# Three turns of attention in another order on TensorE, and one more pair of the first dense stage by the plain product

## The chip, the cores and the metric

The kernel runs on one core of a Trainium2 chip. The metric is device time in microseconds (us), the median of several runs. A profiled execution gives the trace from which all rows below are read. PE is TensorE, ACT ScalarE, DVE VectorE, POOL GpSimd and SP SyncE; of SP only its queue of transfers is used here.

## What is computed

Attention of 2 batches and 12 heads over 448 positions (head size 64) is followed by two dense blocks on 896 tokens:

```
scores = cap * tanh(q @ k.T / sqrt(64) / cap)
x  = softmax(scores) @ v                # (896, 768)
h  = x @ w_in1     # 768 x 2048         first dense stage
x  = (h * cos(h)) @ w_out1              # second
h  = x @ w_in2                          # third
out = (h * sigmoid(h)) @ w_out2         # fourth
```

All in float32; most products are made of three matmuls on operands split into a rounded part and a rest.

## The kernel before

**Attention** works through 12 pairs of heads, one turn each. For pair p, `S_pe(p, t)` (L229) multiplies q and k for chunk t: three chunks of two matmul groups (L241) and a small one, t = 3 (L245). The result lies in one of three buffers named `sc`, taken in rotation, so `S_pe(p, 3)` takes the buffer of `S_pe(p, 0)` and must wait until `S_tanh(p, 0)` has read it. `S_tanh` (L253) and `S_exp` (L259) run on ACT. `PV(p, steps)` (L271, matmuls on L275) multiplies with v, one step for two chunks; `PV_mixed` (L279) handles the small chunk, `PV_sums` (L289, L293) the row sums, for which DVE first adds chunks in `e_add` (L301). The order of each engine is the order of the text: turn p issues S of pair p + 1, then PV of pair p. Before the first turn stand pair 0's scores, four matmuls on zeros (`warm_up`, L347, L349), and two of pair 0's three PV steps. In the last turn there are no scores left: `PV_mixed`, `PV_sums` and then the three PV steps.

**The dense stages** run under a planner (`run_plan`). `gemm_in`, `gemm_out`, `gemm_sums` and `gemm_last` describe tasks with an engine, an assumed cost, a due time and the buffers they take; the planner simulates the engines and writes out the order of each. `MARGIN` multiplies its costs for ACT and DVE, `NORMS` says when the last two pairs of attention are ready, and the argument of `run_plan` says when ACT, DVE and SP come free after TensorE starts on the dense work. These numbers change the order only. An adding transfer of 384 KB is planned with 0.9 us on POOL, 2.46 of moving (384 x 1.024 / 0.16 ns) and 3.7 of fixed delays. All dense matmuls are recorded on L706, most DVE sums on L639, most ACT copies on L636, and additions done by a transfer on L484.

The first stage's 16 columns of weight tiles are handled in 8 pairs. The first `PLAIN` pairs are multiplied plainly (`half_prods`); for the others, `m1` to `m7` form seven products of half-sized blocks, and DVE, or an adding transfer where `S1E[p]` says so, makes sums of the weight blocks:

```
pe(3 * len(js), go, ...)     # half_prods: 3 matmuls for each of 6 row blocks, 4 times a pair
pe(9, go, ...)               # block_prod: 9 matmuls, 7 times a pair
```

`HALF1[p]` names the buffers that the split blocks of pair p lie in. In the second stage (`gemm_out`) four groups of sums of weight tiles are made by `w_sum`, `WE[n]` naming the engine of the n-th: DVE, or the adding transfer from POOL's queue.

Of the kernel before, what the change touches and what calls it, by code (L numbers as in the profile page):

```python
# [28 lines left out]
F32 = mybir.dt.float32  # L29
# [9 lines left out]
def tile_attention_ffn_ffn(  # L39
# [11 lines left out]
    B, H, S, D = shape  # L51
    DM = out.shape[0]
    DFF = w_in1.shape[0] * 128
    P = 128
# [42 lines left out]
    xt = [[Part(f"x{j}_{b}") for b in range(B)] for j in range(KD)]  # L97

    KMAX = KD
    PLAIN = 2  # L100
    FIRST_IN = [b * HP + n for n in range(HP) for b in range(2)]
    wjobs = []
    for w_in, w_out in ((w_in1, w_out1), (w_in2, w_out2)):
# [66 lines left out]
    with ExitStack() as actx:  # L170
# [3 lines left out]
        ps_o = actx.enter_context(tc.tile_pool(name="ps_o", bufs=1, space=PSUM))  # L174
# [22 lines left out]
        def load(p):  # L197
            if p >= NPT:
                return
            t = ap_.tile([P, PAD + QK], F32, tag="raw", name=f"raw{p}", bufs=3)  # L200
            if p == 0:
                cut = PAD + FIRST
                nc.sync.dma_start(t[:, :cut], qkv[p][:, :cut])
                nc.scalar.dma_start(t[:, cut:], qkv[p][:, cut:PAD + QK])
            else:
                (nc.gpsimd if p > 2 else nc.sync).dma_start(t[:, PAD:], qkv[p][:, PAD:PAD + QK])
            raw[p] = t

        def load_v(p):
            if p >= NPT:  # L210
                return
            vf[p] = ap_.tile([P, NCH, D], F32, tag="vf", name=f"vf{p}", bufs=2)
            (nc.gpsimd if p > 1 else nc.sync).dma_start(vf[p].rearrange("p c d -> p (c d)"), qkv[p][:, PAD + QK:])
# [15 lines left out]
        def S_pe(p, t):  # L229
            if p >= NPT:  # L230
                return
            ps = ps_s.tile([P, 2, 512], F32, tag="sc", name=f"sc{p}_{t}")
            sc[p, t] = ps
            h, l = qh.get(p), ql.get(p)
            ops = ((h, h), (h, l), (l, h))
            if t < 3:
                cols = slice(S + t * P, S + (t + 1) * P)
                for m, (kk, qq) in enumerate(ops):
                    for u in range(2):
                        rows = slice(u * D, (u + 1) * D)  # L240
                        nc.tensor.matmul(ps[:, u, :S], kk[rows, cols], qq[rows, :S], start=m == 0, stop=m == 2)  # L241
            else:
                x = raw[p][:, PAD:]
                for c in range(0, P, W):
                    nc.tensor.matmul(ps[c:c + W, 0, :S], x[:, FULL + c:FULL + c + W], x[:, :S], start=True, stop=True)  # L245

        def S_tanh(p, t):
            if p >= NPT:
                return
            if t == 0:  # L250
                e32[p] = ap_.tile([P, NCH, S], F32, tag="e32", name=f"e32_{p}", bufs=2)
            n = 2 if t < 3 else 1
            nc.scalar.activation(out=e32[p][:, 2 * t:2 * t + n, :], in_=sc.pop((p, t))[:, :n, :S], func=AF.Tanh, scale=scap)  # L253
# [9 lines left out]
        def acc(d, p, tag):  # L263
            if p in d:
                return d[p], False
            t = ps_o.tile([P, 512], F32, tag=tag, name=f"{tag}{p}") if p < NPT - 1 or tag == "po" else ps_s.tile([P, 2, 512], F32, tag="sc", name=f"{tag}{p}")[:, 0]
            d[p] = t[:, :S]
            return d[p], True


        def PV(p, steps, last=False):  # L271
            po, first = acc(po_, p, "po")
            for n, t in enumerate(steps):
                for u in range(2):
                    nc.tensor.matmul(po[u * D:(u + 1) * D], vf[p][:, 2 * t + u, :], e32[p][:, 2 * t + u, :],  # L275
                                     start=first and n == 0, stop=last and n == len(steps) - 1)


        def PV_mixed(p, last=False):  # L279
            po, first = acc(po_, p, "po")  # L280
            sm, _ = acc(sm_, p, "sm")
            for u in range(2):
                rows, other = slice(u * D, (u + 1) * D), slice((1 - u) * D, (2 - u) * D)
                e = e32[p][rows, NCH - 1, :]
                nc.tensor.matmul(po[rows], vf[p][rows, NCH - 1, :], e, start=first, stop=last)  # L285
                nc.tensor.matmul(sm[other], ones[rows, Q:], e, start=True, stop=False)  # L286


        def PV_sums(p):  # L289
            sm, _ = acc(sm_, p, "sm")  # L290
            x = e01.pop(p)
            for c, e in enumerate((x[:, 1], e32[p][:, 5, :], x[:, 0], e32[p][:, 4, :])):
                nc.tensor.matmul(sm[c * Q:(c + 1) * Q], ones[:, :Q], e, start=False, stop=True)  # L293
# [3 lines left out]
        def e_add(p):  # L297
            if p >= NPT:
                return
            e01[p] = ap_.tile([P, 2, S], F32, tag="e01", name=f"e01_{p}", bufs=2)  # L300
            nc.vector.tensor_tensor(out=e01[p], in0=e32[p][:, 0:2, :], in1=e32[p][:, 2:4, :], op=ALU.add)  # L301
# [3 lines left out]
        def evac(p):  # L305
            xu[p] = ap2.tile([P, S], F32, tag="xu", name=f"xu{p}", bufs=4)
            nc.vector.tensor_copy(xu[p], po_.pop(p))
# [39 lines left out]
        def warm_up(n, ps):  # L347
            for _ in range(n):
                nc.tensor.matmul(ps, zero[:, :P], zero, start=True, stop=True)  # L349
# [27 lines left out]
        S_exp(0, slice(4, NCH))  # L377
        qk_split(1)
        e_add(0)
        warm_up(4, ps_o.tile([P, 512], F32, tag="sm", name="warm1")[:, :S])  # L380
        PV(0, [0, 1])
        for p in range(NPT):
            load(p + 3)
            if p > 0:
                load_v(p + 1)
            for t in range(3):
                S_pe(p + 1, t)
                S_tanh(p + 1, t)
            S_pe(p + 1, 3)
            S_tanh(p + 1, 3)  # L390
            S_exp(p + 1)
            recip(p - 2)
            if p > 0:
                e_add(p)
            qk_split(p + 2)
            for f, *a in early.get(p, []):
                f(*a)
            norm_mul(p - 3)
            norm_split(p - 3)
            if p < NPT - 1:  # L400
                PV(p, [0, 1, 2] if p else [2])
                PV_mixed(p, True)
                evac(p)
                PV_sums(p)
                evac_sums(p)
            else:
                PV_mixed(p)
                PV_sums(p)
                evac_sums(p)
                PV(p, [0, 1, 2], True)  # L410
                evac(p)
        recip(NPT - 2)
        norm_mul(NPT - 3)
# [52 lines left out]
        return t  # L466

    SPARE = 1000
    MARGIN = 1.01

    def dma(eng, kb, fn, r, w, adds=False, **k):
        rate = 0.16 if adds else 0.38 if kb > 450 else 0.24
# [3 lines left out]
    def act(n, fn, r, w, **k):  # L476
        do("ACT", MARGIN * (90 + 0.84 * n), fn, r, w, **k)

    def dve(n, fn, r, w, one=False, **k):
        do("DVE", MARGIN * (66 + 1.05 * n), fn, r, w, **k)  # L480

# [127 lines left out]
                    if not v.left:  # L609
                        give_buf(v)  # L610

    NORMS = 6900, 9700
    GE, WE, LE = [["DVE", "DMA"][n] for n in (0, 0, 0, 1)], [["DVE", "DMA"][n] for n in (0, 0, 0, 1)], [["DVE", "DMA"][n] for n in (1, 1)]
    FE = "DVE"
    S3E = [["DVE", "DMA"][n] for n in (1, 1, 1, 0, 0, 0, 0, 0)]
    DUE = [220000, 230000, 240000, 250000, 260000, 270000, 280000, 290000, 300000, 310000, 320000, 330000, 1000000000, 1000000000, 1000000000, 1000000000]
    base_s = KF + 4 * (HK + 1)
    base_l = base_s + KF

    S1E = [["DVE", "DMA"][n] for n in (1, 0, 1, 0, 0, 0, 0, 0)]  # L620
    HALF1 = [('half', 'ring'), ('half', 'half'), ('half', 'half'), ('half', 'ring'), ('ring', 'ring'), ('half', 'ring'), ('half', 'half'), ('ring', 'ring')]
    low, high = range(KD - 2), range(KD - 2, KD)
    PLAIN_ORDER = [(0, 0), (1, 0), (2, 0), (0, 1, low), (1, 1, low), (0, 1, high), (1, 1, high), (2, 1)]
    for n in range(3, 2 * PLAIN):
        PLAIN_ORDER += [(n, 0), (n, 1)]
    ORDER1 = []
    for p in range(PLAIN, HP):
        q = p - PLAIN
        ORDER1 += [(1, p), (5, p)] + ([(7, p - 1)] if q else []) + [(2, p), (6, p)] + ([(4, p - 1)] if q else []) + ([(7, p)] if p == HP - 1 else []) + [(3, p)]
# [30 lines left out]
    def convert(i, out, outs, view, due=1e9, pool="raw"):  # L660
# [14 lines left out]
        k = {"due": due}  # L675
        do("ACT", MARGIN * 800, f_word, [], [raw], **k)
        do("ACT", MARGIN * 800, f_scale, [], [raw], **k)
        dve(n, f_join, [raw], outs, **k)

    def split(n, hi, lo, vhi, vlo, src, r, neg=False):  # L680
        if n < 800:
            def go():
# [4 lines left out]
                else:  # L687
                    nc.vector.tensor_copy(vhi(), src())
            t = do("COPY", MARGIN * (90 + 0.84 * n), go, r, [hi])
            t.other = 100 + 0.5 * n  # L690
# [227 lines left out]
    def gemm_in():  # L918
# [14 lines left out]
        for j in range(KD):  # L933
            for b in range(B):
                TX[f"B{j // HK + 1}{b + 1}", j % HK] = made(xt[j][b])
        for p, at in ((NPT - 2, NORMS[0]), (NPT - 1, NORMS[1])):
            x, (_, *pair) = v[p - NP][1], TX["B22", p - NP - HK]
# [14 lines left out]
        def start(p):  # L952
            blk[p], rest[p] = blocks((2 * p, 2 * p + 1), p, Val("dbl", I32), True, S1E[p], HALF1[p])

# [79 lines left out]
        every = range(KD)  # L1034
        ws = [plain(i) for i in range(2 * PLAIN)]
        pts = {}
# [198 lines left out]
    gemm_out()  # L1235
    gemm_sums()
    gemm_last()
    run_plan({"ACT": 2200, "DVE": 4000, "SP": 7500})


# [46 lines left out]
```

## Time and profile before

| | |
|---|---|
| median of 3 runs | 514.46 us (513.86 to 514.7) |
| the profiled execution | 514.24 us |
| its span, first to last instruction | 511.9 us |
| PE busy | 504.6 us (99%) |
| DVE busy | 425.9 us (83%) |
| ACT busy | 404.3 us (79%) |
| POOL busy | 66.5 us (13%) |
| granted clock of TensorE, mean | 0.999 |

Attention takes the first 93 us of the span, the dense stages the rest. The profiled execution spends 2.34 us outside its span. A matmul's recorded end is modelled, so records overlap; what one costs is read from start to start.

### The profile page before, as it was taken

The page shows a single profiled execution, that of the slowest core. Times are in us where ns is not written, and L with a number is a line of the kernel's source. Part 1 is how long each engine was busy: PE and PEld are TensorE (multiplying, and loading weights), DVE is VectorE, ACT ScalarE, POOL GpSimd, SP SyncE. Part 2 cuts the span into 40 slices and gives each one's busy share as a digit, 9 for nine tenths or more (in the row PEclk, how much of TensorE's full clock was granted, in tenths as well). Part 3 has the DMA queues.
Part 4 walks back from the last instruction along what each step waited for, and adds up shares of the span by engine and source line. Part 5 has one row for each costly group of instructions (what it writes and reads, how often), then busy time and mean ns, then how long its engine had stood idle before and what let it go on. Part 6 is the DMA issues. An engine that isn't in the chain of part 4 may idle for free.

```text
span 511.9 us, 7243 instructions
## 1 busy us (share of the span) xinstructions
PE 504.6 (99%) x2634; PEld 419.1 (82%) x2634; DVE 425.9 (83%) x608; ACT 404.3 (79%) x553; POOL 66.5 (13%) x91
## 2 busy tenths in 40 slices
PE   8999999999999999999999999999999999999997
PEld 5344443799999988799999999999999999999996
DVE  5378997999999999999999999776779867965660
ACT  6999998689998889999787588799999655546441
POOL 0144442001000000001401122100000202410000
PEclk9999999999999999999999999999999999999999
DMA  8156464295431355799945383998988943990111
GB/s 313 58 138 178 128 213 136 63 315 154 135 131 63 123 162 209 252 335 280 202 122 148 75 248 67 358 316 292 344 319 289 361 83 64 240 232 13 55 54 54
DMA packets 28134, 93.68 MB, mean 183 GB/s; under 512 B 4600, under 2 KB 10276, under 8 KB 28100
## 3 DMA queue, kind: packets, MB, share of 16 engines
q1 hardware_dynamic: 19488, 70.89, 39.6%
q0 software_dynamic: 8256, 22.03, 20.1%
q8 instruction: 20, 0.33, 0.3%
q10 hardware_dynamic: 356, 0.32, 0.2%
q14 instruction: 14, 0.11, 0.1%
HBM read 72.75 MB, written 10.66 MB: 163 GB/s over the span
## 4 chain that ended last, share of the span: by engine, by line
PE 96%; ACT 2%; issue 1%; DVE 0%
PE bank L706 81%; PE po L275 5%; PE sc L241 4%; PE sm L293 2%; PE sc L245 2%; PE po L285 2%; ACT e L253 1%; PE warm L349 1%; ACT e L259 1%; DVE e L301 0%; DVE zero L358 0%; DVE v L1225 0%; ACT v L636 0%; PE sm L286 0%; DVE sums L320 0%
## 5 line engine op out<-in xcount | busy, mean ns | idle before, releaser
L706 PE MATMUL bank<-v,hl 128*128 128x448 f32 x1494 | 308.7, 366 | 0.0
L706 PEld LDWEIGHTS bank<-v,hl 128*128 128x128 f32 x1494 | 280.5, 188 | 23.9 <-issue 1.1
L639 DVE TENSOR_TENSOR v<-v,v 128x896 fp32r<-128x896 f32 (+4 forms) x111 | 107.6, 991 | 26.3 <-ACT v L636 25.9
L636 ACT ACTIVATE v<-v 128x896 fp32r<-128x896 f32 (+2 forms) x84 | 71.1, 857 | 53.2 <-PE bank L706 47.3
L639 DVE TENSOR_TENSOR hl<-v,hl 128x768 fp32r<-128x768 f32 (+1 forms) x92 | 81.7, 894 | 3.1 <-ACT hl L636 3.0
L636 ACT ACTIVATE hl<-v 128x768 fp32r<-128x768 f32 (+1 forms) x89 | 69.6, 791 | 4.4 <-issue 1.8
L668 ACT ACTIVATE wraw<-wraw 128x768 int32<-128x768 uint8 x61 | 55.3, 914 | 11.9 <-DMA sums<-xs 6.0
L671 ACT ACTIVATE wraw<-wraw 128x768 f32<-128x768 f32 x61 | 55.3, 913 | 0.0
L484 POOL DMA_DIRECT2D v<-v x28 | 26.2, 964 | 205.0 <-ACT wraw L671 108.1
L706 PE MATMUL bank<-v,v 128*128 128x448 f32 x222 | 51.9, 384 | 0.0
L706 PEld LDWEIGHTS bank<-v,v 128*128 128x128 f32 x222 | 41.7, 188 | 6.6 <-issue 3.3
L706 PE MATMUL bank<-x,hl 128*128 128x448 f32 x216 | 45.5, 366 | 0.0
L253 ACT ACTIVATE e<-sc,scap 128x896 f32<-128x896 f32 (+1 forms) x48 | 39.9, 912 | 6.4 <-PE sc L241 6.4
L706 PEld LDWEIGHTS bank<-x,hl 128*128 128x128 f32 x216 | 40.5, 188 | 4.0 <-DVE xs L312 0.7
L674 DVE SCALAR_TENSOR_TENSOR v<-wraw 128x768 int32<-128x768 int32 x42 | 39.6, 951 | 2.5 <-ACT wraw L671 2.4
L636 ACT ACTIVATE v<-bank 128x448 f32<-128x448 f32 (+2 forms) x52 | 27.6, 534 | 13.9 <-PE bank L706 13.8
L259 ACT ACTIVATE e<-e,capt 128x3136 f32<-128x3136 f32 (+2 forms) x13 | 35.2, 2709 | 0.4
L275 PE MATMUL po<-e,vf 128*64 128x448 f32 x144 | 29.4, 540 | 0.6 <-ACT e L259 0.6
L639 DVE TENSOR_TENSOR v<-v 128x384 f32<-128x384 f32 (+1 forms) x46 | 25.5, 559 | 0.2
L275 PEld LDWEIGHTS po<-e,vf 128*64 128x64 f32 x144 | 10.2, 137 | 17.5 <-issue 16.3
L639 DVE TENSOR_TENSOR v<-bank,v 128x448 f32<-128x448 f32 x28 | 16.9, 619 | 9.1 <-PE bank L706 8.9
L314 POOL DMA_DIRECT2D sums<-xs x22 | 17.5, 800 | 50.3 <-DVE sums L320 41.4
(80 smaller groups left out, 460.2 us busy)
## 6 DMA issues: line engine op xcount, KB each, us to landing
wraw<-in_moe_w_out SPq DMA_DIRECT2D x32, 768.0 KB, 5.3
wraw<-in_moe_w_in SPq DMA_DIRECT2D x29, 768.0 KB, 5.4
wd<-wx SPq DMA_DIRECT2D x16, 384.0 KB, 4.5
v<-wd SPq DMA_DIRECT2D x16, 384.0 KB, 7.6
v<-v POOLq DMA_DIRECT2D x12, 384.0 KB, 8.0
raw<-in_qkv POOLq DMA_DIRECT2D x9, 480.0 KB, 4.7
v<-wd POOLq DMA_DIRECT2D x8, 384.0 KB, 6.8
rb<-rs SPq DMA_DIRECT2D x24, 112.0 KB, 3.2
```

The source lines that it names most:

```text
L241: nc.tensor.matmul(ps[:, u, :S], kk[rows, cols], qq[rows, :S], start=m == 0, stop=m == 2)
L253: nc.scalar.activation(out=e32[p][:, 2 * t:2 * t + n, :], in_=sc.pop((p, t))[:, :n, :S], func=AF.Tanh, scale=scap)
L259: nc.scalar.activation(out=e, in_=e, func=AF.Exp, scale=capt)
L275: nc.tensor.matmul(po[u * D:(u + 1) * D], vf[p][:, 2 * t + u, :], e32[p][:, 2 * t + u, :], start=first and n == 0, stop=last and n == len( ...
L314: (nc.gpsimd if p < NPT - 1 else nc.scalar).dma_start(sums[p][:, y], x[y * Q:y * Q + D + 1:D])
L484: dma("POOL", kb, lambda: nc.gpsimd.dma_start(o(), b(), accum_op=ALU.add), r, w, adds=True)
L636: nc.scalar.activation(out=out, in_=src, func=AF.Copy, scale=scale)
L639: nc.vector.tensor_tensor(out=out, in0=a, in1=b, op=op)
L668: nc.scalar.activation(out=b[:, :, 0], in_=b.bitcast(U8)[:, :, 3], func=AF.Copy, scale=1.0 / 32, bias=-0.5 + 1.0 / 64)
L671: nc.scalar.activation(out=w(1).bitcast(F32), in_=w(1).bitcast(F32), func=AF.Prelu, scale=2.0 ** -112, alpha=2.0 ** 32)
L674: nc.vector.scalar_tensor_tensor(out=view(), in0=w(1), scalar=3, in1=w(0), op0=ALU.logical_shift_left, op1=ALU.bitwise_or)
L706: nc.tensor.matmul(bank, x, y, start=first and m == 0, stop=last and m == len(ops) - 1, skip_group_check=True)
```

## The change

Three turns of attention are issued in another order. `S_pe(1, 0)` moves in front of the warm-up ahead of the first turn, and that warm-up has two matmuls instead of four. In turn 1 the first PV step of pair 1 moves in front of `S_pe(2, 3)`. In the last turn the first PV step moves in front of `PV_sums`. In the first dense stage `PLAIN` rises from 2 to 3: pair 2 is multiplied plainly. In the second, the third group of weight sums goes from DVE to the adding transfer. The planner's constants change (`MARGIN`, `NORMS`, the free times), as do the buffers of pair 6, and `S1E[0]`, which neither kernel reads, since pair 0 is plain in both.

```diff
-    PLAIN = 2
+    PLAIN = 3
...
-        warm_up(4, ps_o.tile([P, 512], F32, tag="sm", name="warm1")[:, :S])
+        S_pe(1, 0)
+        warm_up(2, ps_o.tile([P, 512], F32, tag="sm", name="warm1")[:, :S])
         PV(0, [0, 1])
...
             for t in range(3):
-                S_pe(p + 1, t)
+                if p or t:
+                    S_pe(p + 1, t)
                 S_tanh(p + 1, t)
+            if p == 1:
+                PV(p, [0])
             S_pe(p + 1, 3)
...
-                PV(p, [0, 1, 2] if p else [2])
+                PV(p, [2] if p == 0 else [1, 2] if p == 1 else [0, 1, 2])
                 PV_mixed(p, True)
...
                 PV_mixed(p)
+                PV(p, [0])
                 PV_sums(p)
                 evac_sums(p)
-                PV(p, [0, 1, 2], True)
+                PV(p, [1, 2], True)
...
-    MARGIN = 1.01
+    MARGIN = 1.0
...
-    NORMS = 6900, 9700
-    GE, WE, LE = [["DVE", "DMA"][n] for n in (0, 0, 0, 1)], [["DVE", "DMA"][n] for n in (0, 0, 0, 1)], [["DVE", "DMA"][n] for n in (1, 1)]
+    NORMS = 7700, 10500
+    GE, WE, LE = [["DVE", "DMA"][n] for n in (0, 0, 0, 1)], [["DVE", "DMA"][n] for n in (0, 0, 1, 1)], [["DVE", "DMA"][n] for n in (1, 1)]
...
-    S1E = [["DVE", "DMA"][n] for n in (1, 0, 1, 0, 0, 0, 0, 0)]
-    HALF1 = [('half', 'ring'), ('half', 'half'), ('half', 'half'), ('half', 'ring'), ('ring', 'ring'), ('half', 'ring'), ('half', 'half'), ('ring', 'ring')]
+    S1E = [["DVE", "DMA"][n] for n in (0, 0, 1, 0, 0, 0, 0, 0)]
+    HALF1 = [('half', 'ring'), ('half', 'half'), ('half', 'half'), ('half', 'ring'), ('ring', 'ring'), ('half', 'ring'), ('ring', 'ring'), ('ring', 'ring')]
...
-    run_plan({"ACT": 2200, "DVE": 4000, "SP": 7500})
+    run_plan({"ACT": 3000, "DVE": 4800, "SP": 8300})
```

## Rows read from the trace of the kernel before

**Rows 1.** Busy time by stretch: stretch, length, engines' busy us (instructions), PE clock, DMA.

```profile
core 0: us, PE busy (x) PEld busy (x) DVE busy (x) ACT busy (x) POOL busy (x), PEclk, DMA share, GB/s
0.00:24.84 24.84, 22.23 (x135) 10.97 (x135) 11.21 (x19) 20.01 (x18) 3.58 (x12) 1.00 0.53 191
...
93.20:122.50 29.30, 29.30 (x147) 27.16 (x146) 27.74 (x50) 25.54 (x40) 1.86 (x2) 1.00 0.64 195
122.50:198.00 75.50, 75.50 (x369) 69.08 (x368) 75.16 (x125) 68.41 (x115) 1.72 (x2) 1.00 0.42 133
198.00:304.00 106.00, 106.00 (x507) 95.09 (x507) 104.15 (x127) 89.21 (x126) 12.15 (x14) 1.00 0.70 203
```

**Rows 2.** Waits of PE: line, who released it, us in total, times, longest us.

```profile
PE sm L293 <- DVE e L301: 1.0, 1, 1.0
...
PE sc L245 <- ACT e L253: 0.6, 1, 0.6
```

**Rows 3.** Chain that ended last: start us, us, what (dense stages).

```profile
93.25 415.11 PE bank L706 x2022
```

**Rows 4.** Timeline of ACT, opening turns: start, us, line, operation, [idle before <-releaser].

```profile
6.18 1.90 ACT L253 ACTIVATE e<-sc,scap 128x896 f32<-128x896 f32 x2 [3.50 <-PE sc L241]
...
18.84 0.99 ACT L253 ACTIVATE e<-sc,scap 128x896 f32<-128x896 f32 x1
...
22.18 2.91 ACT L259 ACTIVATE e<-e,capt 128x3136 f32<-128x3136 f32 x1
25.00 0.88 ACT L132 ACTIVATE wx<-wraw 128x768 f32<-128x768 f32 x1
25.78 1.00 ACT L253 ACTIVATE e<-sc,scap 128x896 f32<-128x896 f32 x1
...
32.76 1.90 ACT L253 ACTIVATE e<-sc,scap 128x896 f32<-128x896 f32 x2 [0.73 <-PE sc L241]
```

**Rows 5.** Timeline of PE, opening turns.

```profile
9.96 1.72 PE L275 MATMUL po<-e,vf 128*64 128x448 f32 x8 [0.62 <-ACT e L259]
...
18.91 0.37 PE L241 MATMUL sc<-qh,ql 64*128 64x448 f32 x2
19.88 0.97 PE L245 MATMUL sc<-raw 128*64 128x448 f32 x4 [0.61 <-ACT e L253]
...
26.59 0.37 PE L241 MATMUL sc<-qh,ql 64*128 64x448 f32 x2
26.89 0.97 PE L245 MATMUL sc<-raw 128*64 128x448 f32 x4
```

**Rows 6.** Timeline of PE, last turn of attention.

```profile
88.39 0.54 PE L286 MATMUL sm<-e,ones 64*64 64x448 f32 x1
89.88 0.96 PE L293 MATMUL sm<-e,ones 128*32 128x448 f32 x8 [0.96 <-DVE e L301]
90.77 2.48 PE L275 MATMUL po<-e,vf 128*64 128x448 f32 x12
```

**Rows 7.** Timeline of PE, dense stages (neighbouring rows of one form merged).

```profile
93.18 29.45 PE L706 MATMUL bank<-x,hl 128*128 128x448 f32 x144
122.47 3.81 PE L706 MATMUL bank<-x,v 128*128 128x448 f32 x18
...
376.69 131.65 PE L706 MATMUL bank<-v,hl 128*128 128x448 f32 x648
```

**Rows 8.** Groups of DVE instructions by shape: count, busy us, mean ns, idle before.

```profile
L639 DVE TENSOR_TENSOR hl<-v,hl 128x768 fp32r<-128x768 f32 x79 | 74.9, 951 | 3.1 <-ACT hl L636 3.0
...
L639 DVE TENSOR_TENSOR v<-v,v 128x768 f32<-128x768 f32 x12 | 11.3, 951 | 0.0
...
L639 DVE TENSOR_TENSOR bank<-bank,v 128x448 f32<-128x448 f32 x12 | 7.5, 627 | 0.3 <-PE bank L706 0.2
...
L639 DVE TENSOR_TENSOR hl<-v,hl 128x384 fp32r<-128x384 f32 x13 | 7.0, 550 | 0.0
```

**Rows 9.** Transfers by queue: count, KB each, median us from issue to landing.

```profile
v<-v POOLq DMA_DIRECT2D x12, 384.0 KB, 8.0
```

## The prediction

> **What bounds the kernel now.** I read the busy time by stretch first. From 93.2 us on TensorE is busy for the whole of each stretch, with DVE beside it at 102.90 of 104.8 us in the first dense stage and 104.15 of 106 in the second; in the first 24.84 us TensorE works for 22.23 and ACT for 20.01 [rows 1]. The clock granted to TensorE is 1.00 in these rows, the 2.4 GHz level.
>
> The waits of TensorE come next, because its busy time is built from modelled ends. Two that matter are 0.6 us for tanh in the opening and 1.0 us for the sum of DVE in the last turn of attention [rows 2]. None is in the dense stages: the chain that ended last runs through their 2,022 matmul records for 415.11 us without a break [rows 3].
>
> Then I checked that no wait is hidden between overlapping records, by the distance of starts. The first 144 matmuls take 122.47 - 93.18 = 29.29 us, 0.2034 each; the 648 of the last product stages take 131.65 us, or about 131.5 without the tail of the last modelled record, 0.2029 each [rows 7]. The pace is the same whether DVE is at 98% or not. So the dense stages cost their number of matmuls times 0.2034 us, and only attention has waits to give back.
>
> **The opening.** TensorE waits before the small chunk of pair 2, at 19.88: tanh of its first chunk, whose buffer it takes, runs from 18.84 to 19.83, so the release takes 0.05 us [rows 4, 5]. Unhindered, the small chunk starts 0.30 us after the last large one (26.59 to 26.89) [rows 5], here at 18.91 + 0.30 = 19.21; 0.67 us are lost. A PV step costs 0.76 us: three last 2.48 us, two last 1.72 [rows 5, 6]. Put at 19.21, where its exponential is done (tanh follows it on ACT at 18.84), it fills the hole and ends at 19.97, 0.09 us past the release. Seen from there, turn 1 ends 0.76 - 0.09 = 0.67 us earlier.
>
> But what is late next? ACT. It stands idle until 6.18 and the first time it waits for scores again is the 0.73 us before 32.76 [rows 4]: from 6.18 to 32.03 its work never pauses for TensorE. Nothing that TensorE does sooner in this time makes ACT faster. One turn later the small chunk of pair 3 needs the tanh that starts at 25.78, behind the exponential from 22.18 and a weight-scaling copy of 0.88 us, and ends at 26.78 [rows 4]. With the release of 0.05 us TensorE may start at 26.83; it started at 26.89 [rows 5]. So all but 0.06 us of the gain turns into a wait there, and I take **-0.06 us** (bounds 0 and -0.67). Moving `S_pe(1, 0)` and leaving out two warm-up matmuls is worth nothing for the same reason: the 0.62 us before 9.96 is a wait for ACT [rows 5], scores that are ready sooner lie before ACT until it is free, and the warm-ups lie in that wait. Were that cover gone, two matmuls cost 0.41 us.
>
> **The last turn.** The row sums start 0.96 us late, for DVE's sum [rows 2, 6]. The records go from 88.39 to 89.88, start to start; a PV step of 0.76 us fits into 0.96 and leaves 0.20 for the switch to it and from it [rows 6]. `PV_sums` starts as before, behind an unchanged chain on DVE, and two PV steps follow instead of three: **-0.76 us** (bounds -0.66, with a switch of 0.1 us paid, and -0.80, a third of the 2.41 us from 90.77 to 93.18). The copy of the sums, their transfer and the last norms keep their times, and the dense work starts 0.8 us nearer to them.
>
> **The third plain pair.** Plain, a pair takes 4 x 18 = 72 matmuls; by seven products of nine it takes 63. Nine more at 0.2034 us are **+1.83 us** (bounds 1.83 by the 0.2029 above, and 1.85 by the mean over the whole chain, 415.11 / 2,022 = 0.2053, which holds the few slower matmuls on unsplit float32). There is no idle time of TensorE in which they could hide [rows 1, 3].
>
> For these nine it matters whether a matmul costs what the rows show. The Trainium skill (TensorE: Matmul & The Clock Gate, section "Back-to-back issue gap") gives columns / 2.4 + 2.5 ns for a warm matmul, 189 ns for 448 columns. By that the nine would cost 1.70 us and the sum would be 0.13 us lower; the rows at the 2.4 GHz level show 0.2034 [rows 7], and I go by them.
>
> DVE is relieved. By blocks, pair 2 needs three rests of 0.951 us, a short one of 0.550 and two combinations of 0.627 (its block sums were transfers): 4.66 us; plain, it needs two rests, 1.90 us [rows 8]. That is 2.76 us off an engine that had 1.9 us to spare in the stage [rows 1], while the stage grows. So an earlier start of TensorE by 0.82 us does not by itself make DVE late. I count it as nothing: relief of an engine nobody waits for.
>
> **The third group of weight sums** leaves DVE, four additions of 0.951 us [rows 8], and becomes four transfers of 384 KB that take 8.0 us to land [rows 9]. Behind them on POOL's queue stand the next group's additions, already transfers. They can start when the previous product's weight sums have read the tile, and are due a product later, 72 x 0.2034 = 14.6 us. That covers a landing, so I take nothing. If the cover is gone: the planner's constants give 0.9 + 2.46 + 3.7 = 7.1 us for one, against 8.0 measured, so up to 0.9 us late each, 0.9 to 3.6 us for four.
>
> **Only order.** `MARGIN`, `NORMS`, the free times and the buffers of pair 6 add no instruction. A plan that believes ACT and DVE 1% quicker can put a task late; over the 104 us of a stage that is 1.0 us. Nothing is taken, and it belongs to the same rival.
>
> **Sum.** -0.06 - 0.76 + 1.83 = +1.01 us. The profiled execution took 514.24 us, so 515.25 by its own scale; it lies 0.22 us under the median of 514.46, which gives **515.5 us**. A measurement of this kernel tells about 0.2%, 1.03 us, from no change, so the forecast sits on that bound.
>
> **The rivals.**
>
> *A task comes late in the first or second dense stage* (0.14). For it: DVE is at 98% in both [rows 1], the order is new, and the moved sums take 8.0 us to land. Against: DVE has 2.76 us less to do in the first and 3.8 less in the second. It costs 0.9 to 3.6 us: 516.4 to 519.1, likeliest 517.
>
> *The opening keeps its gain* (0.08), the case that ends not slower. It holds if ACT gets past the tanh at 25.78 sooner, which needs a pause of ACT before it that the merged rows hide. Then -0.67 stands for -0.06: 514.9. It decides as soon as ACT is 0.3 us sooner. Against: ACT's pieces adjoin to hundredths.
>
> *Small waits hidden between matmuls shrink with DVE's load* (0.05). Going by 0.2029 against 0.2034 us in some 1,500 matmuls, 0.75 us: 514.7.
>
> *DVE, not TensorE, sets the pace of the first two stages* (0.03), the case that ends faster. Then nine matmuls cost nothing and 2.76 + 3.8 us come off: 514.46 - 0.82 - 6.56 = 507.1. For it: 98% busy. Against: TensorE's pace is 0.203 in the last stages too, where DVE has slack, and no record waits for DVE there [rows 3, 7]. The Trainium skill (Perfetto Trace Analysis, section "Identifying the Most-Contended Engine") says that matmul occupancy is a poor measure and names the most occupied engine as the one to relieve; by that rule this case would be likelier. The distance of starts speaks against it.
>
> *TensorE's clock falls after the shortened warm-up* (0.02). The two PV steps behind it, 1.72 us [rows 5], would take as much again at 1.2 GHz: 517.2. Against: the wait in front of them, 0.62 us, shrinks rather than grows, as scores take more time than the two matmuls left out.
>
> **How the numbers follow.** The forecast (0.68) reaches from 515.1 to 515.9 by its bounds and the spread of the runs, half of it on each side of 515.49: 0.34 same, 0.34 slower. With the cases: slower 0.34 + 0.14 + 0.02 = 0.50, same 0.34 + 0.08 + 0.05 = 0.47, faster 0.03. The range, 514.6 to 517.0, takes in the gains kept and most of the stall, and leaves out the far ends.
>
> **What would show it.** In the new profile the wait at 19.88 should be gone and a wait of about 0.6 us for tanh should stand before the small chunk of pair 3, near 26.83. The row sums of the last turn should start at about 89.8 after a wait under 0.3, and the first dense matmul at about 92.4 instead of 93.18. The dense chain should hold 2,031 records and last 416.9 us; longer, or with a row of TensorE waiting for DVE or for an adding transfer, and the stall rival is right. DVE's busy time should fall by about 6.5 us with no effect. I am wrong if the dense matmuls lie closer than 0.2025 us or the chain is cut.

## The result and the profile after

The changed kernel takes **517.91 us** (517.62 to 518.71, 4 runs) against 514.16 us for the kernel before in the same comparison (513.74 to 514.7, 4 runs). The ratio is 1.0069 [1.0057, 1.0082], so the change costs 3.75 us where I had predicted +1.01. The profiled execution took 517.78 us, its span grew from 511.9 to 515.9 us.

The first lines of the page after: TensorE is busy 3.9 us longer, DVE 4.5 us less.

```profile
span 515.9 us, 7244 instructions
...
PE 508.5 (99%) x2641; PEld 420.0 (81%) x2641; DVE 421.4 (82%) x599; ACT 402.9 (78%) x549; POOL 66.5 (13%) x91
```

Busy time by stretch after, for most of the first dense stage and for the second (columns as in [rows 1]):

```profile
122.50:198.00 75.50, 75.50 (x373) 69.66 (x372) 71.25 (x117) 65.75 (x110) 0.00 (x0) 1.00 0.33 108
198.00:304.00 106.00, 106.00 (x504) 94.36 (x503) 100.65 (x122) 90.08 (x125) 15.90 (x18) 1.00 0.76 218
```

DVE has 3.9 us less to do in the first of these stretches and 3.5 less in the second, and the clock granted to TensorE is still 1.00. So neither more work on DVE nor the clock explains a longer time.

The waits of TensorE after (columns as in [rows 2]):

```profile
PE sc L245 <- ACT e L253: 1.2, 2, 0.6
PE bank L711 <- DVE xs L312: 0.4, 1, 0.4
```

The 1.0 us for DVE's sum [rows 2] is gone, the wait for tanh is there twice instead of once, and there is a new wait of 0.4 us, of a dense matmul for `xs`, DVE's copy of the row sums. The opening shows where the second tanh wait lies (timelines of TensorE and of ACT after):

```profile
19.27 0.97 PE L275 MATMUL po<-e,vf 128*64 128x448 f32 x4
20.07 0.92 PE L245 MATMUL sc<-raw 128*64 128x448 f32 x4
...
26.91 0.97 PE L245 MATMUL sc<-raw 128*64 128x448 f32 x4 [0.59 <-ACT e L253]
```
```profile
25.08 0.89 ACT L132 ACTIVATE wx<-wraw 128x768 f32<-128x768 f32 x1
```

The PV step fills the hole before the small chunk of pair 2, and the 0.6 us return before the small chunk of pair 3, at 26.91 against 26.89 before [rows 5]. The last turn of attention (timeline of TensorE):

```profile
88.91 0.97 PE L275 MATMUL po<-e,vf 128*64 128x448 f32 x4
89.94 0.96 PE L293 MATMUL sm<-e,ones 128*32 128x448 f32 x8
90.82 1.72 PE L275 MATMUL po<-e,vf 128*64 128x448 f32 x8
92.95 1.28 PE L711 MATMUL bank<-x,hl 128*128 128x448 f32 x5 [0.41 <-DVE xs L312]
```

The chain that ended last, from the end of attention on (start us, us, what):

```profile
89.88 0.86 DVE hl L163
90.74 0.55 DVE xv L334
...
91.31 0.41 DVE x L341
...
91.74 0.63 DVE x L342
92.36 0.55 DVE xs L312
...
92.95 419.38 PE bank L711 x2031
```

The PV step takes the place of the wait [rows 6] as predicted, but the first dense matmul waits: it takes the PSUM buffer in which the last row sums lay, and DVE copies them out only after a weight rest and the norm of pair 8. Dense work starts at 92.95, 0.23 us earlier than before [rows 7], where I had -0.82 for opening and last turn together.

How early the first tanh starts differs from trace to trace, by up to half a microsecond, and shifts all that follows. So tenths are read inside each trace (ACT and TensorE after, then TensorE before):

```profile
6.26 1.01 ACT L253 ACTIVATE e<-sc,scap 128x896 f32<-128x896 f32 x1 [3.57 <-PE sc L241]
82.78 0.97 PE L245 MATMUL sc<-raw 128*64 128x448 f32 x4
```
```profile
82.73 0.97 PE L245 MATMUL sc<-raw 128*64 128x448 f32 x4
```

From the first tanh to the small chunk of pair 3 it is 26.91 - 6.26 = 20.65 us, against 26.89 - 6.18 = 20.71 before [rows 4, 5]. From the last small chunk to the first dense matmul it is 92.95 - 82.78 = 10.17 us, against 93.18 - 82.73 = 10.45. So the opening gives 0.06 us and the last turn 0.28.

The larger part is in the last line. 2,031 records take 419.38 us, 4.27 more than 2,022 took [rows 3]. Nine matmuls were to cost 1.83; **2.4 us remain with no wait at all**. The last product stages hold the same 648 matmuls as before [rows 7] and need no sums of weight blocks. They are longer all the same (timeline after):

```profile
378.54 133.78 PE L711 MATMUL bank<-v,hl 128*128 128x448 f32 x648
```

Without the tail of the last record (0.36 us, the length of a record that stands alone), the distance of starts is (133.78 - 0.36) / 647 = 0.2062 us; before, it was (131.65 - 0.36) / 647 = 0.2029 [rows 7]. One stretch of these 648 settles what does not cause it: from 464.3 to 477.1 no transfer runs (busy time by stretch after, columns as in [rows 1], and the timeline of the same stretch):

```profile
464.30:477.10 12.80, 12.80 (x64) 11.62 (x63) 6.93 (x7) 7.93 (x11) 0.00 (x0) 1.00 0.00 0
```
```profile
464.01 13.39 PE L711 MATMUL bank<-v,hl 128*128 128x448 f32 x64
```

Sixty-four matmuls at (13.39 - 0.36) / 63 = 0.2068 us, with DMA at 0.00, POOL idle, DVE at half load and the clock at 1.00. The single starts show **two paces**: distances of 203, 202, 203, 199, 207 ns in turn (0.2027 us on average), or 206 and 207 ns throughout (0.2067 us). Counted by these patterns, 167 of 2,010 dense matmuls of the kernel before run at the slow pace and 828 of 2,019 in the changed one, from 406.6 us on all of them (the twelve on unsplit float32 make two records each, hence 2,022 and 2,031). 661 more at 0.004 us are 2.6 us. Such counts are each of one profiled execution.

### The profile page after: what moved, and what is told of

The parts are those of the page before. It is cut to its first block, busy times and chain, and to the rows that moved or that the text cites. A ratio compares the mean times of both kernels' runs of the same rounds, so it can differ in the third digit from the quotient of the medians.

```text
span 515.9 us, 7244 instructions
## 1 busy us (share of the span) xinstructions
PE 508.5 (99%) x2641; PEld 420.0 (81%) x2641; DVE 421.4 (82%) x599; ACT 402.9 (78%) x549; POOL 66.5 (13%) x91
## 4 chain that ended last, share of the span: by engine, by line
PE 95%; ACT 2%; DVE 1%; DMA 1%; issue 0%
PE bank L711 81%; PE po L275 5%; PE sc L241 4%; PE sc L245 2%; PE sm L293 2%; PE po L285 2%; ACT e L253 1%; DMA raw<-in_qkv 1%; ACT e L259 1%; DVE e L301 0%; ACT wx L132 0%; DVE hl L163 0%; DVE ql L225 0%; DVE xs L312 0%; DVE x L342 0%
## 5 line engine op out<-in xcount | busy, mean ns | idle before, releaser
L711 PEld LDWEIGHTS bank<-v,hl 128*128 128x128 f32 x1476 | 277.2, 188 | 25.5 <-issue 0.6
L644 DVE TENSOR_TENSOR v<-v,v 128x896 fp32r<-128x896 f32 (+4 forms) x103 | 100.8, 997 | 31.5 <-ACT v L641 31.3
L641 ACT ACTIVATE v<-v 128x896 fp32r<-128x896 f32 (+2 forms) x81 | 68.7, 857 | 55.5 <-PE bank L711 49.3
L711 PE MATMUL bank<-x,hl 128*128 128x448 f32 x315 | 65.5, 366 | 0.4 <-DVE xs L312 0.4
L711 PEld LDWEIGHTS bank<-x,hl 128*128 128x128 f32 x315 | 59.1, 188 | 5.9 <-DVE xs L312 1.2
L711 PE MATMUL bank<-v,v 128*128 128x448 f32 x204 | 48.3, 387 | 0.0
L711 PEld LDWEIGHTS bank<-v,v 128*128 128x128 f32 x204 | 38.3, 188 | 6.9 <-issue 3.7
L679 DVE SCALAR_TENSOR_TENSOR v<-wraw 128x768 int32<-128x768 int32 x40 | 37.7, 953 | 4.3 <-ACT wraw L676 4.2
L968 ACT ACTIVATE v<-v,quarter 128x448 f32<-128x448 f32 x32 | 21.3, 671 | 1.9 <-DVE v L966 1.8
```

The costliest lines, as they stand in the source:

```text
L641: nc.scalar.activation(out=out, in_=src, func=AF.Copy, scale=scale)
L644: nc.vector.tensor_tensor(out=out, in0=a, in1=b, op=op)
L679: nc.vector.scalar_tensor_tensor(out=view(), in0=w(1), scalar=3, in1=w(0), op0=ALU.logical_shift_left, op1=ALU.bitwise_or)
L711: nc.tensor.matmul(bank, x, y, start=first and m == 0, stop=last and m == len(ops) - 1, skip_group_check=True)
L968: act(S, lambda: nc.scalar.activation(out=r(), in_=r(), func=AF.Sin, scale=2.0 * math.pi, bias=quarter), [table], w)
```

## The experiments

Each time stands beside runs of the kernel before made with it on the same chip: 514.39 us for the first group, 514.29, 514.27 and 514.57 for the next three. The theory at the outset was that the pace depends on where in SBUF (the core's on-chip memory) the operands lie; the rivals were the number of matmuls, the order of attention, and tasks of DVE or transfers that come late.

**The parts alone.** `e1_attention` is the kernel before with the attention order of the change:

```diff
+        S_pe(1, 0)
+        warm_up(2, ...)
...
+            if p == 1:
+                PV(p, [0])
...
+                PV(p, [0])
                 PV_sums(p)
```

> The kernel before with the three turns of attention reordered, nothing else: two plain pairs, the planner's constants of before. Both theories: the opening gives at most 0.06 us (ACT bounds it) and the dense work starts about 0.2 us sooner, not 0.76, because the first dense matmul waits for the copy of the row sums on DVE; about 514.0. Theory of two paces (a dense matmul takes 0.2027 or 0.2067 us, and the pace is thrown over when the moving operand lies in the topmost buffers of SBUF): the dense chain can come out anywhere from 414.5 to 417 us though its instructions and addresses are those of before. Theory of hidden waits on DVE and transfers under the plan: the dense chain stays at 415.1 us, or grows by 0.2 as TensorE comes sooner to an unchanged plan.

Measured: 513.69 us (513.27 to 514.62, 12 runs), ratio 0.9986 [0.9977, 0.9995]. `e2_plain` is the kernel before with one number changed:

```diff
-    PLAIN = 2
+    PLAIN = 3
```

> The kernel before with three plain pairs instead of two, nothing else: attention and the planner's constants of before. Number of matmuls alone: nine more, +1.83 us, about 516.0, dense chain 416.9. Two paces: the same plus or minus the share of matmuls that fall into the slow pace, which other addresses decide, 515.5 to 518. Hidden waits: DVE has less to do than before, so 516.0 or a little under.

Measured: 515.71 us (515.59 to 516.21, 7 runs), ratio 1.0025 [1.0014, 1.0035]. The chain rows of the two:

```profile
92.78 415.05 PE bank L711 x2022
```
```profile
93.81 416.98 PE bank L706 x2031
```

Nine matmuls cost 416.98 - 415.11 = 1.87 us, as priced. The parts come to -0.70 and +1.32; the whole change to +3.75. Slow matmuls are few in both, 177 and 219, so neither part alone brings the long slow stretches.

**Where do the operands lie?** In the memory map of the compiled program five buffers for split blocks, `gr0` to `gr4`, lie at the top of SBUF from byte 211,424 of each partition, 3,584 bytes each: at 224 modulo 256 (the remainder of the byte address divided by 256). All other dense operands lie at 96 modulo 256. In the records before and after, nearly every longer stretch of slow pace ends where a matmul takes one of the five, and begins within a few matmuls of leaving them; one of 17 matmuls in the changed kernel, from 205.7 us, lies between matmuls on unsplit float32 instead. By the same map the matmuls that are left again in this way have one of the five as their moving operand; stretches that take them as weights alone (from 310.4 us after) stay fast. Two things could matter, the region or the position modulo 256. `e3_top` puts the raw weights above them, which moves the five down by 18,432 bytes (72 x 256), in the same order of instructions:

```diff
-    wx = wpool.tile([P, 2, KMAX, P], I32, name="wx")
+    wx = wtop.tile([P, 2, KMAX, P], I32, name="wx")   # wtop: a pool on the right side
```

> The changed kernel, same order of every engine, with the staging buffers of the raw weights put at the top of SBUF, so that the five buffers that lay there from byte 211,424 of a partition on lie below 210,912. Two paces: no matmul is in the slow pace, the dense chain falls from 419.4 to about 415.2 us and the time from 517.9 to about 514. Hidden waits on DVE and transfers: the order is the same, so is the time, 517.9. Number of matmuls alone: 517.9 too.

Measured: 517.6 us (515.93 to 518.16, 6 runs), ratio 1.0053 [1.0035, 1.007]. The last 648 matmuls (timeline):

```profile
378.41 133.78 PE L712 MATMUL bank<-v,hl 128*128 128x448 f32 x648
```

The same 133.78 us, and 827 slow matmuls at the same places. **The region was the wrong theory.** Two of the six runs took only 516.0 us; no trace of them was kept. `e5_align` leaves 128 bytes free at the top, so that the five lie at 96 modulo 256 as well; `e7_shift256` is the control with 256 bytes, and `e10_shift192` puts them at 32, 64 bytes from the others:

```diff
+    skew = ctx.enter_context(tc.tile_pool(name="skew", bufs=1, side="right"))
+    skew.tile([P, 32], F32, name="skew")      # 64 in e7_shift256, 48 in e10_shift192
```

> The changed kernel with 128 bytes of a partition left free at the top of SBUF, so that the five upper buffers move down by 128 bytes; same order. Theory of alignment (the pace is thrown over when the address of an operand changes from 96 to 224 by 256, as in the five upper buffers, or back): all dense operands then lie at 96 by 256, no matmul is slow, the dense chain falls from 419.4 to about 415.3 us, the time from 517.9 to about 514. Theory that the order itself sets the pace, since moving the five buffers by 18 KB changed nothing: 517.9, the slow stretches where they were.

> The control: the changed kernel with 256 bytes left free instead of 128, so that every buffer moves but its address by 256 stays. Alignment: the slow stretches stand where they were, about 517.9. If leaving any room helped, it would be 514 as in the run with 128.

> The changed kernel with 192 bytes left free, so that the upper buffers lie at 32 by 256, the others at 96: they differ by 64 bytes instead of 128. If the 128-byte part of the address alone counts, nothing is thrown over: 514.7, as with 128 bytes free. If every difference counts, slow stretches come back, 515.5 to 518.5.

Measured: **514.69 us** (514.15 to 515.42, 11 runs), ratio 1.0006 [0.9997, 1.0016] with 128 bytes; 518.39 us (518.16 to 518.55, 5 runs), 1.0075 [1.006, 1.0089] with 256; 518.89 us (518.67 to 519.2, 4 runs), 1.0089 [1.0075, 1.0102] with 192. The chain and the timeline of the first (the last line is the stretch without transfers shown above), then the 648 matmuls of the second and the chain of the third:

```profile
93.26 416.04 PE bank L713 x2031
```
```profile
377.80 131.49 PE L713 MATMUL bank<-v,hl 128*128 128x448 f32 x648
...
463.94 13.34 PE L713 MATMUL bank<-v,hl 128*128 128x448 f32 x65
```
```profile
379.20 133.78 PE L713 MATMUL bank<-v,hl 128*128 128x448 f32 x648
```
```profile
93.19 420.22 PE bank L713 x2031
```

With 128 bytes the same instructions in the same order take 3.34 us less in the dense chain, no matmul is slow, and in the stretch without transfers 65 matmuls fit where 64 did. With 256 bytes the slow ones are back, 828 at the same places; with 192 there are 1,080. So, in the changed kernel, a difference of 128 or of 64 bytes modulo 256 brings the slow pace, equal positions take it away, and a shift by a whole 256 changes nothing. That much is shown, by every run of these three and of the changed kernel. That bit 7 of the address alone decides, my idea after the first two, fell with the third.

**What else aligning gives.** `e6_align_before` is the kernel before with the same 128 bytes, `e8_best` adds the attention order and an earlier copy of the last row sums (as in `e4_sums` below), `e9_attention_align` adds the attention order alone.

> The kernel before with the same 128 bytes left free. Alignment: its 167 slow matmuls and the small delays around changes of alignment go, 2.1 us above the fast pace become about 0.5: 1.4 to 1.6 us less, about 512.8. Order: 514.4, unchanged.

> Two plain pairs and the planner's constants of before, the reordered attention, the copy of the last row sums ahead of the norm of pair 8, and 128 bytes left free. Alignment: 1.5 us for the pace and 0.7 for the last turn, 512.2. Order: 513.7, that of the reordered attention alone. Hidden waits on DVE and transfers: the 0.7 us come back as a wait in a later stage, 512.9 or 514.4.

> Two plain pairs and the planner's constants of before, attention reordered as in the change, and 128 bytes left free at the top of SBUF. Alignment: no change of pace inside the dense stages; if they begin at the fast pace, as in the changed kernel with 128 bytes free, 514.7 - 1.83 = 512.9 or a little under; if they begin slow, as in the run without the wait before the first dense matmul, up to 2 us more. That the reordered attention and the alignment share one gain: 513.7.

Measured: 513.98 us (512.78 to 516.59, 12 runs), 0.9993 [0.9979, 1.0007]; 514.15 us (512.9 to 517.83, 12 runs), 0.9996 [0.998, 1.0011]; **512.78 us** (512.55 to 513.23, 6 runs), 0.997 [0.9958, 0.9982]. The last is the fastest of all, 1.5 us under the kernel before and about 5.1 us under the changed one. The first dense matmuls of the second and of the third show what holds the second back (timelines):

```profile
92.33 30.02 PE L717 MATMUL bank<-x,hl 128*128 128x448 f32 x144
```
```profile
93.07 29.45 PE L713 MATMUL bank<-x,hl 128*128 128x448 f32 x144 [0.41 <-DVE xs L314]
```

The second starts 0.74 us earlier, and then runs at the slow pace from 92.8 to 191.0 us, although all operands share one position. (30.02 - 0.36) / 143 is 0.2074 us, against 0.2034. So equal positions do not choose the fast pace: in these records a stretch keeps the pace in which it began, and a change of position is one way to get into the other. The slow stretch of the second ends at matmuls on unsplit float32, and behind such ones 43 slow matmuls begin in the third and in the aligned kernel before. The latter has no others, 43 instead of 167, but starts 0.44 to 0.49 us apart at 126.3 and 137.4 us that no row of waits names; its gain is not measurable.

**The wait for the row sums.** `e4_sums` is the changed kernel with DVE's copy of the last row sums ahead of the weight rest and the norm of pair 8:

```diff
-            for f, *a in early.get(p, []):
-                f(*a)
-            norm_mul(p - 3)
-            norm_split(p - 3)
...
                 PV_sums(p)
                 evac_sums(p)
+                for f, *a in early.get(p, []):
+                    f(*a)
+                norm_mul(p - 3)
+                norm_split(p - 3)
```

> The changed kernel, with DVE's copy of the last row sums in front of the last weight rest and the norm of pair 8 instead of behind them. The wait of the first dense matmul (0.4 us by the row, started at 92.95) goes and the dense work starts at about 92.4: 0.5 us less, about 517.4, if the paces fall as in the changed kernel. Rival: the norm of pair 8 comes 0.6 us later and a later matmul waits for it: 517.9.

Measured: 518.03 us (517.02 to 519.09, 6 runs), 1.0069 [1.0055, 1.0083]. The wait of 0.41 us is gone and the dense work starts at 92.30, 0.65 us earlier (0.48 read from the last small chunk, at 82.61), with only 223 slow matmuls. By the memory map it runs the same dense matmuls in the same order on the same addresses as the changed kernel, which had 828: **order and positions together do not fix the pace either.** But its waits, its timeline and its chain show others:

```profile
PE bank L715 <- DVE v L648: 1.3, 2, 0.7
...
PE bank L715 <- DVE v L697: 1.0, 1, 1.0
PE bank L715 <- ACT bank L645: 0.3, 1, 0.3
```
```profile
311.52 0.65 PE L715 MATMUL bank<-v,v 128*128 128x448 f32 x2 [0.99 <-DVE v L697]
```
```profile
303.18 7.54 DMA wx<-wx
310.81 0.56 DVE v L697
...
325.22 9.52 DMA wd<-wx
334.86 0.96 DVE wx L683
335.82 0.87 DVE hl L648
337.28 175.82 PE bank L715 x864
```

TensorE runs into 2.6 us of real waits, behind transfers of 7.54 and 9.52 us. The aligned kernel, which starts the dense work at 93.26 and runs at the fast pace throughout, has none of these waits. So it is the earlier start, or the norm of pair 8 that now comes later on DVE, that uses up the cover of the transfers; the two are not told apart.

**The two attention edits apart.** `e11_last_turn` is the kernel before with the last turn's edit alone; `e12_opening` is the changed kernel with the weight-scaling copies that stood in turn 1 on ACT put into turn 2:

```diff
+                PV(p, [0])            # e11_last_turn
                 PV_sums(p)
...
+        late0 = {0: 1, 1: 2, 2: 2}    # e12_opening
-                early.setdefault(turn + at, []).append(step)
+                early.setdefault(turn + (at if w else late0.get(at, at)), []).append(step)
```

> The kernel before with the edit of attention's last turn alone. ACT bounds the opening: dense work starts within 0.1 us of where it starts with all three turns reordered, 92.8 to 92.9, and the time is that of the run with attention reordered, 513.7. If the opening's edits bring something: 0.3 to 0.7 us later than that.

> The changed kernel with the weight-scaling copy of turn 1 (0.88 us of ACT) put into turn 2, where ACT has 0.7 us to spare. ACT bounds the opening: the wait of 0.6 us before the small chunk of pair 3 goes, all that follows in attention is about 0.6 us sooner and the dense work starts at about 92.3; the time falls by 0.6 if the paces fall as before, to 517.3. If ACT doesn't bound it, the dense work starts at 92.95 as it did.

Measured: 513.95 us (513.38 to 517.51, 12 runs), 0.9997 [0.9983, 1.0011]; 517.69 us (515.98 to 518.67, 6 runs), 1.0061 [1.0045, 1.0078]. In the timelines of the two:

```profile
92.81 1.48 PE L707 MATMUL bank<-x,hl 128*128 128x448 f32 x6 [0.41 <-DVE xs L312]
```
```profile
26.64 0.97 PE L245 MATMUL sc<-raw 128*64 128x448 f32 x4
...
402.68 109.92 PE L712 MATMUL bank<-v,hl 128*128 128x448 f32 x531 [0.34 <-ACT v L642]
```

The last turn alone starts the dense work at 92.81 instead of 93.18, with the same 0.41 us wait; its time cannot be told from no change. Inside the traces (TensorE of the first, ACT of the second):

```profile
82.64 0.97 PE L245 MATMUL sc<-raw 128*64 128x448 f32 x4
```
```profile
6.62 1.01 ACT L253 ACTIVATE e<-sc,scap 128x896 f32<-128x896 f32 x1 [3.93 <-PE sc L241]
```

The last turn takes 92.81 - 82.64 = 10.17 us, as in the changed kernel: 0.28 us gained, and the rest of the 0.37 is an earlier first tanh. With the copy moved, the wait at 26.91 is gone: the small chunk starts 26.64 - 6.62 = 20.02 us behind the first tanh instead of 20.65, 0.63 earlier, which shows that ACT held it. Dense work starts at 92.65, as much earlier by the same reading. But it ends at 402.68 + 109.92 = 512.60, against 92.95 + 419.38 = 512.33, so 0.57 us are lost again in it, 0.34 of them in a wait at 402.68.

**Which edit brings the slow pace?** `e13_both` is the kernel before with the attention order and `PLAIN = 3`, all other lines as before; `e14_pair6` and `e15_wsum` are the changed kernel with one line set back each:

```diff
+    HALF1 = [..., ('half', 'half'), ('ring', 'ring')]         # e14_pair6
...
+    WE = [["DVE", "DMA"][n] for n in (0, 0, 0, 1)]            # e15_wsum
```

> Both measured parts together, the attention order and the third plain pair, with the planner's constants, the sums' engine and the buffers of the kernel before. If the loss beyond the nine matmuls comes from the lines that only re-order the dense work (constants, third group of sums, buffers of pair 6), the parts add: -0.70 and +1.32 us, so about 515.0 (514.4 to 515.7), and the last 648 matmuls take 131.5 to 131.8 us. If the two parts hinder each other, the time is that of the whole change, 517.3 to 518.3, with 133.8 us for the last 648.

> The whole change with the buffers of pair 6 as before. They decide how often the odd-address buffers are met in the first stage. If the slow pace at the end hangs on what happens in the last stages, it stays: 517.3 to 518.3, last 648 in 133.8 us. If the buffers of pair 6 start it by shifting the order, about 515.3 (514.8 to 516.0) and 131.7 us.

> The whole change with the third group of weight sums on DVE again, as before. If giving it to the adding transfer costs time by itself, or its order sets the slow pace at the end, the last 648 matmuls take 131.5 to 131.8 us and the time is about 515.3 (514.8 to 516.0). If it plays no part: 517.3 to 518.3 and 133.8 us.

Measured: 515.87 us (515.44 to 517.53, 12 runs), 1.0028 [1.0015, 1.004]; 518.54 us (516.93 to 520.15, 6 runs), 1.008 [1.0058, 1.0103]; 516.15 us (515.8 to 519.83, 12 runs), 1.0035 [1.0019, 1.005]. The last 648 matmuls of the first and the third:

```profile
378.54 131.64 PE L711 MATMUL bank<-v,hl 128*128 128x448 f32 x648
```
```profile
379.21 131.69 PE L711 MATMUL bank<-v,hl 128*128 128x448 f32 x648
```

Without the planner's constants, the third group of sums and the buffers of pair 6 the change costs +1.30 us; they add some 2.4. Setting back the third group of sums removes most of that, and the last stages are fast again. The times lie 0.2 us above the bands I had given for the first and third, and runs of one program scatter (515.8 to 519.83 for the third). The second is inconclusive: its six runs spread over 3.2 us, and the profiled one was the fastest of them, fast at the end and slow from 93.4 to 144.4.

## Why the prediction was wrong

**The step that failed** is "So the dense stages cost their number of matmuls times 0.2034 us". I had taken the mean over 144 matmuls and over 648 and found them equal; both means lay near the fast pace (what lifts the first to 0.2034 is one distance of 0.31 us, from the first matmul to the second), and the slow stretches of the kernel before were only 167 matmuls, 0.7 us. The price of a matmul is not a constant of its shape: 0.2027 or 0.2067 us, and an edit that adds no matmul can switch it for hundreds of them. The experiment with 128 bytes shows it: 3.34 us of the dense chain went with the addresses alone. That is more than the 2.4 that no wait explained, since the kernel before had slow stretches too.

**Nine more matmuls, +1.83 us:** right, 1.87 in the dense chain with `PLAIN` alone.

**The third group of sums and the planner's lines, 0 us:** wrong in size and in kind. I had looked for a transfer that lands late. The adding transfers did become longer (queue rows after, against 8.0 us in [rows 9]):

```profile
v<-v POOLq DMA_DIRECT2D x16, 384.0 KB, 10.2
```

but TensorE waits for none of them in the changed kernel. Undoing the line and aligning the buffers both take most of the loss away. That the line does it through the order in which buffers at the two positions are met is argued, not shown: `e4_sums` keeps that order and has 223 slow matmuls. The rival of a late task is thus not what happened; it appeared in `e4_sums`, when TensorE came earlier.

**The last turn, -0.76 us:** the mechanism was right, the size was not. The row sums started at 89.94 without a listed wait, as foreseen. I wrote that the copy of the sums kept its time and did not ask who needs it: the first dense matmul, 0.41 us. Read inside the traces, the edit gives 0.28 us, alone and in the whole change.

**The opening, -0.06 us:** right, 20.65 us instead of 20.71. The wait of 0.59 us stands where I had put it, and moving the copy from ACT takes it away.

**DVE's relief, no effect:** right in effect. It was 4.5 us instead of about 6.5.

**The clock and DVE as the bound:** neither happened; the granted clock is 1.00 in the stretches shown, and TensorE became slower while DVE had less to do.

The Trainium skill (TensorE: Matmul & The Clock Gate, section "Back-to-back issue gap") gives columns / 2.4 + 2.5 ns as the distance of warm matmuls, by estimate 189 ns for 448; it means a matmul taken alone, which the prediction left out, and puts those of a stream of 512 columns closer still. Here the same columns cost 202.7 or 206.7 ns in a stream, and the operands' addresses have a part in which of the two, so the measurement decides twice over. The Trainium skill (SBUF — State Buffer, section "Who interferes with whom") says that TensorE shares no SBUF port with other engines or with DMA; the stretch from 464.3 us, slow with the DMA share at 0.00, agrees insofar as no transfer is needed for the slow pace.

**What stays open:** why a difference of 64 or 128 bytes changes the pace, what makes a stretch begin slow when all positions are equal, as in `e8_best`, why the same order on the same addresses gives 828 slow matmuls once and 223 in `e4_sums`, and why the last switch of buffers leaves the changed kernel slow (from 406.6 us, behind three matmuls from 405.5 that take one of the five as the moving operand) where that of the kernel before, at 396.9, leaves it fast. The records point to the moving operand; no run separates its position from the weights'.

## What to carry to other kernels

On an engine that never waits, do not price work by a mean duration alone: look at the distances of single starts, and if there are two, count how many operations run at each before and after. Lay out all operands of a long matmul stream at one position modulo 256 bytes and look at the pace again: this cost 128 bytes, took 3.2 us off the changed kernel and nothing measurable off the kernel before. When an edit brings one engine forward, ask of its first new instruction which buffer it takes and who empties it, and which transfers have just lost their cover.

## What the runs showed of the hardware

Dense matmuls of 448 columns on split float32 operands come 0.2027 or 0.2067 us apart at the same granted clock, and keep a pace for hundreds of instructions: 416.04 us against 419.38 and 420.22 us for the same dense chain. Buffers 128 or 64 bytes apart modulo 256 brought the slow pace to 828 and 1,080 of 2,019 matmuls; with none apart the same order had no slow one, 514.69 us against 517.91. Neither is a rule by itself: a kernel with all positions equal began with 475 slow matmuls, and another with the buffers 128 bytes apart had 223.
